# Attention, routed experts and a dense softplus layer on one core: a branch past the weight split of an expert block whose predecessor had the same expert

## The chip, the cores and the metric

One Trainium2 chip; the kernel runs on one core of it. The metric is the device time of one execution in microseconds (us), the median of repeated runs. The kernel before takes 573.91 us (three runs, 573.8 to 574.29).

## What is computed

Three stages follow each other; all inputs are float32.

```
a = attention(rotate(q), rotate(k), v)             # 2 batches, 8 heads, 576 tokens, 64 dims
x = a as [1152 tokens, 512]
e = argmax(norm(x) @ norm(expert_emb).T / tau)     # one of 8 experts per token
x[t] = gate[t] * (relu(x[t] @ w1[e]) @ w2[e])      # w1: 8 x 512 x 1024, w2: 8 x 1024 x 512
out = softplus(x @ w_in) @ w_out                   # 512 -> 2048 -> 512
```

For the inputs of the measurement the eight experts receive 109, 200, 97, 486, 143, 31, 85 and 1 tokens.

## The kernel before

TensorE multiplies fp32r numbers. To keep float32 accuracy every operand is split into a high part (its value rounded to fp32r, a copy on ScalarE) and a low part (the difference, on VectorE); each product is then three matmuls: high by high, high by low, low by high.

The expert stage (some 194 to 363 us of the span) sorts the tokens by expert into blocks of 128 rows. Every expert has at least one block and one more for each further 128 tokens; blocks of one expert are neighbours. With the counts above there are 13 blocks (`NU`, line 913), of experts 0, 1, 1, 2, 3, 3, 3, 3, 4, 4, 5, 6, 7. On the chip VectorE computes this sequence: `eid` is the expert of a block, and `chg` (line 299) is 1 where a block's expert differs from that of the block before it. So `chg` is 0 for blocks 2, 5, 6, 7 and 9.

Per block n the work is: gather the 128 rows, transpose and split them (`x_t`, `x_ev`), 24 matmuls of the first layer in four chunks of the contraction (`layer1`, line 1001), relu on ScalarE (line 1008), transpose and split the hidden rows (`h_t`, `h_ev`, line 985), 24 matmuls of the second layer in four chunks (`layer2`, line 1030), scale by the gate (`y_row`, line 1037) and scatter the rows to memory (`y_put`, line 1040).

Weights: the two layers have four raw chunks each of 128 x 1024 floats (`raws_w`, line 934), one buffer per layer and chunk. `fetch_w(n, l, c)` (line 943) issues on SyncE's queue the 512 KB transfer of chunk c of layer l for block n. It carries the condition `chg[n] > 0`, so for a block that repeats the expert no bytes move and the raw buffer keeps its data. `split_hi` (line 959) takes a buffer of the eight in pool `wp` and writes the high part on ScalarE (line 962); `split_lo` (line 964) writes the low part on VectorE (line 966) and then issues the fetch of the same chunk for block n + 1, which may overwrite the raw chunk as soon as both halves have read it. The splits are done for every block, whether its raw chunk is new or not.

All engines run in an order written out by hand. Blocks 0 to 3 are interleaved with the routing in straight code; from n = 4 the loop `run` (line 1066) holds a steady pattern. One turn n is, in the order of each engine's queue: split the hidden rows of block n - 1 (`h_ev`), `layer1(n)`, split the second layer's weights of block n - 1, `relu(n)`, the rows of block n + 1 (`x_t`, `x_ev`), `y_out(n - 2)`, split the first layer's weights of block n + 1, `layer2(n - 1)`, from n = 8 the transposes of one tile of finished rows for the next stage (`y_t`, line 903, whose load `y_load`, line 896, SyncE issues a turn earlier behind that turn's weight fetches), `h_t(n)`, and `between(n)`. For n = 4 to 7 `between` also decodes one chunk of the dense layer's weights on ScalarE and VectorE (`decode`, line 861), and fetches another. The lines of the loop that split weights:

```
                if n0 < n < n1:
                    for c in range(4):
                        split_w(n - 1, 1, c)
...
                    for c in range(4):
                        if (n + 1, 0, c) not in wts:
                            split_w(n + 1, 0, c)
```

After the loop a branch of all engines (lines 1292 and 1302) jumps past the code for a 14th to 16th block, which isn't needed here; then the dense stage runs.

Of the kernel before, what the change touches and what calls it, by code (L numbers as in the profile page):

```python
# [13 lines left out]
F32R = mybir.dt.float32r  # L14
# [11 lines left out]
P = 128  # L26
B, H, S, D = 2, 8, 576, 64
NT, DM = B * S, H * D
E, FF, DFF = 8, 1024, 2048
# [61 lines left out]
def f(ap):  # L91
    return ap.bitcast(F32)
# [3 lines left out]
def moe_kernel(ctx: ExitStack, tc: tile.TileContext, q, k, v, emb, tau, w1, w2, w_in, w_out, rope, tab, out):  # L96
    nc = tc.nc
# [51 lines left out]
    chg = rt.tile([P, NBLK], I32, name="chg")  # L149
# [699 lines left out]
    NB = NBLK  # L849
# [63 lines left out]
    NU = E + 5  # L913
# [5 lines left out]
    if True:  # L919
        wr = ectx.enter_context(tc.tile_pool(name="wr", bufs=1, reuse_waits="tile"))  # L920
        xg_ = ectx.enter_context(tc.tile_pool(name="xg", bufs=1, reuse_waits="tile"))
        wp = ectx.enter_context(tc.tile_pool(name="wp", bufs=8, reuse_waits="tile"))
# [5 lines left out]
        xgs = [xg_.tile([P, DM], F32R, name=f"xg{i}") for i in range(3)]  # L928
        for t in xgs:
            G.memset(f(t), 0.0)  # L930
        regs, wts, xts, hts, hs, yps = {}, {}, {}, {}, {}, {}

        wr.tile([P, 528], F32, name="below")
        raws_w = {(l, c): wr.tile([P, FF], F32, name=f"raw{l}{c}") for l in range(2) for c in range(4)}
# [8 lines left out]
        def fetch_w(n, l, c):  # L943

            if n >= NB:
                return
            if l == 0:
                src = w1.rearrange("e (k p) f -> e k p f", p=P)
            else:
                src = w2.rearrange("e (c p r) d -> e c p (r d)", p=P, r=2)  # L950
            if n == 0:
                SY.dma_start(raws_w[l, c], src[0, c])
                return
            if n not in regs:
                regs[n] = [SY.value_load(t[0:1, n:n + 1], min_val=0, max_val=m) for t, m in ((eid, E - 1), (chg, 1))]
            e, new = regs[n]
            SY.dma_start(raws_w[l, c], src[ds(e, 1), c].rearrange("e p f -> (e p) f"), cond=(new > 0) if (n, l) != (1, 0) else (e < 1))

        def split_hi(key):
            raw = raws_w[key[1:]]  # L960
            wt = wts[key] = wp.tile([P, 2, FF], F32R, tag="w", name="wt")
            A.copy(wt[:, 0], raw)  # L962

        def split_lo(key, eng=None, ahead=True):
            raw, wt = raws_w[key[1:]], wts[key]
            (eng or V).tensor_tensor(wt[:, 1], raw, f(wt[:, 0]), op=ALU.subtract)  # L966
            if ahead:
                fetch_w(key[0] + 1, *key[1:])

        def split_w(*key):  # L970
            split_hi(key)
            split_lo(key)

        def gather(n):
            G.indirect_dma_start(f(xgs[n % 3])[:, :], None, xs[:, :], bass.IndirectOffsetOnAxis(idx[:, n:n + 1], axis=0), bounds_check=NT - 1, oob_is_err=False)
# [11 lines left out]
        def x_t(n):  # L987
            return four(lambda k: xgs[n % 3][:, k * P:(k + 1) * P], F32R)

        def x_ev(n, pt, tag="xt"):  # L990
            xt = xts[n] = xe.tile([P, 2, 4, P], F32R, tag=tag, name="xt", bufs=1)
            hi_lo(xt, pt)

        def layer1(n):
            xt = xts.pop(n)
            ph = hs[n] = [ps_x.tile([P, 512], F32, tag="x", name="ph") if n == 1 else ps_h.tile([P, 512], F32, tag="h", name="ph") for _ in range(2)]
            for c in range(4):
                wt = wts.pop((n, 0, c)) if n else firsts.pop(c)
                for i in range(2):
                    for a, r in ((0, 0), (0, 1), (1, 0)):  # L1000
                        T.matmul(ph[i], lhsT=xt[:, a, c], rhs=wt[:, r, 512 * i:512 * i + 512] if n else wt[r][:, 512 * i:512 * i + 512], start=(c == 0 and a == 0 and r == 0), stop=(c == 3 and a == 1))  # L1001
                yield

        def relu(n):
            ph = hs.pop(n)
            h = hs[n] = xe.tile([P, FF], F32, tag="hr", name="hr", bufs=1)
            for i in range(2):
                A.activation(h[:, 512 * i:512 * i + 512].rearrange("p (k r q) -> p k r q", k=2, r=2), ph[i].rearrange("p (k q r) -> p k r q", k=2, r=2), AF.Relu)

        def h_t(n):  # L1010
            h = hs.pop(n)
            return [four(lambda k: h[:, 512 * i + P * k:512 * i + P * k + P]) for i in range(2)]

        def h_ev(n, pts, mid=lambda: None):
            ht = hts[n] = [xe.tile([P, 2, 4, P], F32R, tag=f"ht{i}", name="ht", bufs=1) for i in range(2)]
            for i in range(2):
                hi_lo(ht[i], pts[i])
                if i == 0:
                    mid()

        def layer2(n):
            ht = hts.pop(n)
            py = yps[n] = ps_y.tile([P, DM], F32, tag="y", name="py")
            for c in range(4):
                wt = wts.pop((n, 1, c))
                for r in range(2):
                    rhs = wt.rearrange("p a (r d) -> p a r d", r=2)[:, :, r]
                    k = 2 * (c % 2) + r
                    for a, s in ((0, 0), (0, 1), (1, 0)):
                        T.matmul(py, lhsT=ht[c // 2][:, a, k], rhs=rhs[:, s], start=(c == 0 and r == 0 and a == 0 and s == 0), stop=(c == 3 and r == 1 and a == 1))  # L1030
                yield
# [14 lines left out]
        def y_out(n):  # L1046
            y_row(n)
            y_put(n)
# [17 lines left out]
        def run(n0, n1, between=lambda n: None, early=lambda n: None, early_t=lambda n: lambda: None, pts=None):  # L1066

            for n in range(n0 if pts is None else n0 + 4, n1 + 1):
                if n + 2 < n1:
                    gather(n + 2)  # L1070
                if pts:
                    h_ev(n - 1, pts)
                    pts = None
                if n == n1:
                    split_w(n - 1, 1, 3)
                    if n0 + 2 <= n:
                        y_out(n - 2)
                    between(n)
                if n < n1:
                    for _ in layer1(n):  # L1080
                        pass
                if n0 < n < n1:
                    for c in range(4):
                        split_w(n - 1, 1, c)
                if n < n1:
                    relu(n)
                if n + 1 < n1:
                    px = x_t(n + 1)
                if n + 1 < n1:
                    x_ev(n + 1, px)  # L1090
                if n0 + 2 <= n < n1:
                    y_out(n - 2)
                if n + 1 < n1:
                    for c in range(4):
                        if (n + 1, 0, c) not in wts:
                            split_w(n + 1, 0, c)
                elif n < n1:
                    between(n)
                    split_w(n, 1, 0)
                l2 = layer2(n - 1) if n0 < n <= n1 else iter(())  # L1100
                if n + 1 == n1:
                    for _ in range(2):
                        next(l2, None)
                    h_ev(n, h_t(n), lambda: [split_w(n, 1, c) for c in (1, 2)])
                for _ in l2:
                    pass
                ev = early_t(n)
                if n + 1 < n1:
                    pts = h_t(n)
                ev()  # L1110
                if n == n1:
                    y_row(n - 1)
                if n < n1:
                    early(n)
                if n + 1 < n1:
                    between(n)

        def between(n):
            if n == 1:
                pgat = bank(2).rearrange("p a e -> p (a e)")  # L1120
                for b in range(B):
                    at_places(pgat, b, "row", "gm")
                V.tensor_copy(gates, pgat)
                xctx.close()
                ypool = ctx.enter_context(tc.tile_pool(name="ypool", bufs=1, side="right", reuse_waits="tile"))
                yr3.extend(ypool.tile([P, DM + 1], F32R, name=f"yr{i}") for i in range(4))
                ypools.append(ypool)
                for t in yr3:
                    G.memset(f(t), 0.0)
                yts[0] = ypool.tile([P, 2, 4, TOK_PASSES[0][1] * P], F32R, name="yt0")  # L1130
            if n in (2, 3):
                for i in range(2 * n - 4, 2 * n - 2):
                    fetch(*ORDER[i], raw_)
            if 4 <= n < 8:
                decode((*ORDER[n - 4], dec))
                fetch(*ORDER[n], raw_)
            if n == NU - 1:
                split(0, 0)
                tc.mark_branch_hint_location("extra", T.value_load(extra[0:1, 0:1], min_val=0, max_val=1), [mybir.EngineType.PE])
            if n == NU:  # L1140
                split(0, 1)
# [333 lines left out]
```

## Time and profile before

| | us |
|---|---|
| median of three runs | 573.91 |
| the profiled execution | 574.03 |
| its span | 572.3 |
| TensorE busy | 544.2 |
| VectorE busy | 448.8 |
| ScalarE busy | 440.1 |
| GpSimd busy | 202.6 |

The span runs from the first to the last instruction of the profiled execution; its own time is 1.73 us longer. Busy times are of the engines' own instructions and run beside each other; the share over the whole span hides that the stages have different limits, so the expert loop has to be read by itself.

### The profile page before, as it was taken

What the parts mean: (1) busy time and instruction counts of PE and PEld (TensorE: products, weight loads), DVE (VectorE), ACT (ScalarE), POOL (GpSimd) and SP (SyncE); (2) the same over time, 40 slices, a digit from 0 to 9 for tenths busy, and PEclk for the clock granted to TensorE, in tenths of its full rate; (3) what the DMA queues carried; (4) which work ended last, traced back from release to release, by engine and by line L of the source; (5) the groups of instructions that cost most, each with busy time, mean ns of one, the idle gap of its engine ahead of it and who ended that gap; (6) DMA issues with size and microseconds to landing.
All of it is one profiled execution on the core that took longest, in us unless ns stands there. A gap on an engine that the chain in (4) does not pass through costs nothing. (4 is left out here: it accounts for less than half of the span.)

```text
span 572.3 us, 10066 instructions
## 1 busy us (share of the span) xinstructions
PE 544.2 (95%) x3361; PEld 477.2 (83%) x3361; DVE 448.8 (78%) x747; ACT 440.1 (77%) x838; POOL 202.6 (35%) x314
## 2 busy tenths in 40 slices
PE   6799999999999999998999999899999999999995
PEld 6689899999988888887778888797889999888994
DVE  6788887878977779989999998687877766787243
ACT  4787878887775599799998988788877877676550
POOL 7999999849731420332222412300000000000033
PEclk9899999999999999999999999999999999999999
DMA  5405200061143655982539895453332222000012
GB/s 143 123 2 151 67 1 3 0 221 38 38 169 116 199 163 174 316 300 71 216 102 333 290 377 174 133 191 102 107 112 74 77 80 71 33 1 2 0 74 92
DMA packets 37431, 70.61 MB, mean 123 GB/s; under 512 B 8306, under 2 KB 24050, under 8 KB 37248
## 3 DMA queue, kind: packets, MB, share of 16 engines
q1 hardware_dynamic: 34400, 62.66, 33.1%
q0 software_dynamic: 2800, 7.09, 3.6%
q8 instruction: 28, 0.46, 0.3%
q10 hardware_dynamic: 176, 0.18, 0.2%
q14 instruction: 27, 0.22, 0.1%
HBM read 91.14 MB, written 8.13 MB: 173 GB/s over the span
## 5 line engine op out<-in xcount | busy, mean ns | idle before, releaser
L966 DVE TENSOR_TENSOR wt<-raw,wt 128x1024 fp32r<-128x1024 f32 x100 | 116.4, 1221 | 5.8 <-ACT wt L962 5.8
L1336 PE MATMUL ph<-yt,wt 128*128 128x320 f32 (+1 forms) x576 | 105.4, 336 | 2.5 <-ACT r__5876 L1348 1.4
L1383 PE MATMUL po<-wt,g 128*128 128x512 f32 x432 | 103.6, 391 | 0.0
L1336 PEld LDWEIGHTS ph<-yt,wt 128*128 128x128 f32 x576 | 93.5, 188 | 11.8 <-ACT r__5876 L1348 1.8
L962 ACT CAST wt<-raw 128x1024 fp32r<-128x1024 f32 x100 | 98.8, 1066 | 5.5 <-DMA raw<-in_moe_w_dram 5.5
L1383 PEld LDWEIGHTS po<-wt,g 128*128 128x128 f32 x432 | 80.4, 188 | 16.7 <-ACT g L1367 0.3
L1030 PE MATMUL py<-wt,ht 128*128 128x512 f32 x312 | 75.7, 395 | 3.8 <-DVE wt L966 3.8
L1400 POOL DMA_INDIRECT out_dram<-acc,otok x9 | 9.6, 1067 | 186.2 <-DVE acc L1397 185.6
L1030 PEld LDWEIGHTS py<-wt,ht 128*128 128x128 f32 x312 | 57.5, 188 | 16.6 <-DVE wt L966 5.1
L1001 PE MATMUL ph<-wt,xt 128*128 128x512 f32 x288 | 69.1, 394 | 0.0
L543 ACT ACTIVATE p<-sc,nm 128x576 f32<-128x576 f32 x72 | 54.0, 750 | 11.6 <-DVE nm L537 10.7
L1001 PEld LDWEIGHTS ph<-wt,xt 128*128 128x128 f32 x288 | 53.1, 188 | 10.6
L537 DVE TENSOR_REDUCE nm<-sc 128x1 f32<-128x576 f32 x72 | 54.1, 752 | 3.1 <-PE sc L533 1.9
L556 ACT CAST ph<-tp 128x512 fp32r<-128x512 f32 (+1 forms) x80 | 42.8, 547 | 13.5 <-PE tp L549 13.0
L533 PE MATMUL sc<-kt,qt 128*128 128x288 f32 x256 | 50.4, 319 | 0.8 <-ACT p L543 0.4
L567 DVE TENSOR_TENSOR pl<-tp,ph 128x512 fp32r<-128x512 f32 (+1 forms) x80 | 49.5, 628 | 0.1
L379 POOL TENSOR_TENSOR t<-qk,ropet 128x256 f32<-128x256 f32 x61 | 43.7, 744 | 10.6 <-DMA qk<-in_q_dram 10.2
L549 PE MATMUL tp<-idf,p 128*128 128x128 f32 x288 | 44.8, 278 | 1.8 <-DVE jz L233 0.6
L1367 ACT CAST g<-e 128x512 fp32r<-128x512 f32 (+2 forms) x33 | 21.6, 658 | 29.6 <-PE po L1383 20.2
L1368 DVE TENSOR_TENSOR g<-e,g 128x512 fp32r<-128x512 f32 (+2 forms) x33 | 24.3, 740 | 23.7 <-ACT g L1367 23.5
L594 PE MATMUL po<-ph,vs 128*128 128x288 f32 x128 | 36.4, 307 | 2.2 <-DVE p L435 1.3
L533 PEld LDWEIGHTS sc<-kt,qt 128*128 128x128 f32 x256 | 36.7, 192 | 1.8 <-ACT p L543 1.1
(246 smaller groups left out, 1001.7 us busy)
## 6 DMA issues: line engine op xcount, KB each, us to landing
raw<-in_moe_w_dram SPq DMA_DIRECT2D x116, 512.0 KB
raw<-in_moe_w_in_dram SPq DMA_DIRECT2D x16, 512.0 KB
raw<-in_moe_w_out_dram SPq DMA_DIRECT2D x16, 512.0 KB
yr<-ys SPq DMA_DIRECT2D x9, 256.5 KB
qk<-in_k_dram SPq DMA_DIRECT2D x8, 256.0 KB
qk<-in_q_dram SPq DMA_DIRECT2D x8, 256.0 KB
vv<-in_v_dram SPq DMA_DIRECT2D x8, 256.0 KB
xs<-xrow SPq DMA_DIRECT2D x1, 1024.0 KB
```

Of the source, the lines that this page charges most:

```text
L379: eng.tensor_tensor(t[:, i, g], x4[:, i, g], ropet[:, m, 0:4].unsqueeze(2).to_broadcast([P, 4, 2, 32]), op=ALU.mult)
L533: T.matmul(sc[:, n, 0:288], lhsT=w, rhs=r, start=(x == 0), stop=(x == len(mm) - 1))
L537: V.tensor_reduce(nm, tiles['sc', t][:, :, 0:288], axis=AX.XY, op=ALU.max, negate=True)
L543: A.activation(p.rearrange("p (n t) -> p n t", n=2), tiles.pop(('sc', t))[:, :, 0:288], AF.Exp, bias=tiles.pop(('nm', t)), accum_out=head( ...
L549: T.transpose(tp[:, x], p[:, x * P:x * P + P], idf)
L567: V.tensor_tensor(hd['pl'][:, :, sl], tp[:, :, x * w:x * w + w], f(hd['ph'][:, :, sl]), op=ALU.subtract)
L962: A.copy(wt[:, 0], raw)
L966: (eng or V).tensor_tensor(wt[:, 1], raw, f(wt[:, 0]), op=ALU.subtract)
L1001: T.matmul(ph[i], lhsT=xt[:, a, c], rhs=wt[:, r, 512 * i:512 * i + 512] if n else wt[r][:, 512 * i:512 * i + 512], start=(c == 0 and a == ...
L1030: T.matmul(py, lhsT=ht[c // 2][:, a, k], rhs=rhs[:, s], start=(c == 0 and r == 0 and a == 0 and s == 0), stop=(c == 3 and r == 1 and a == 1))
L1336: T.matmul(phs[i][:, 0:n1 - n0], lhsT=wt[:, a, k], rhs=yts[p][:, r, k, n0:n1], start=(k == 0 and a == 0 and r == 0), stop=(k == 3 and a == 1))
L1383: T.matmul(outs[i][c], lhsT=g[:, a, c * P:c * P + P], rhs=wt[:, r], start=(first and a == 0 and r == 0), stop=(last and a == 1))
```

## The change

A block with `chg` 0 uses the split weights of its predecessor. The eight split buffers get fixed places, one per layer and chunk (`held`), where before they rotated. In the loop the two calls go through `split_new`: it loads `chg[n]` into a register of VectorE and of ScalarE (once per block), and both engines branch on it past the four copies and the four subtractions of that layer. The four fetches for block n + 1 now stand behind the branch in program order instead of one behind each chunk. The branch stands for blocks 3 to 11 in the second layer and 5 to 12 in the first; the straight code ahead of the loop and the last block's second layer split as before.

```diff
@@ split_hi @@
         def split_hi(key):
             raw = raws_w[key[1:]]
-            wt = wts[key] = wp.tile([P, 2, FF], F32R, tag="w", name="wt")
+            home = (0 if key[0] in (NU - 1, NU, NB - 1) else key[1], key[2])
+            if home not in held:
+                held[home] = wp.tile([P, 2, FF], F32R, tag="w", name="wt")
+            wt = wts[key] = held[home]
             A.copy(wt[:, 0], raw)
@@ behind split_w @@
+        def split_new(n, l, cs):
+
+            if n >= NU or (n, l) in ((0, 1), (1, 0)):
+                for c in cs:
+                    split_w(n, l, c)
+                return
+            for c in cs:
+                wts[n, l, c] = held[l, c]
+            if n not in news:
+                news[n] = nc.values_load(chg[0:1, n:n + 1], engines=[mybir.EngineType.DVE, mybir.EngineType.Activation], min_val=0, max_val=1)
+            with tc.If(news[n] > 0, preferred_fallthrough_block=True):
+                for c in cs:
+                    split_hi((n, l, c))
+                    split_lo((n, l, c), ahead=False)
+            for c in cs:
+                fetch_w(n + 1, l, c)
@@ run @@
                 if n0 < n < n1:
-                    for c in range(4):
-                        split_w(n - 1, 1, c)
+                    split_new(n - 1, 1, range(4))
...
                 if n + 1 < n1:
-                    for c in range(4):
-                        if (n + 1, 0, c) not in wts:
-                            split_w(n + 1, 0, c)
+                    split_new(n + 1, 0, range(4))
```

## Rows read from the trace of the kernel before

**Rows 1.** The page: span, busy time of each engine, and one costly group of instructions.

```profile
span 572.3 us, 10066 instructions
...
PE 544.2 (95%) x3361; PEld 477.2 (83%) x3361; DVE 448.8 (78%) x747; ACT 440.1 (77%) x838; POOL 202.6 (35%) x314
...
L962 ACT CAST wt<-raw 128x1024 fp32r<-128x1024 f32 x100 | 98.8, 1066 | 5.5 <-DMA raw<-in_moe_w_dram 5.5
```

**Rows 2.** Block periods by window (loop n = 4 to 9): engines' busy time (x instructions), clock, DMA share, GB/s.

```profile
240.28:252.45 12.17, 12.17 (x64) 10.16 (x61) 10.11 (x12) 10.38 (x15) 5.05 (x6) 1.00 1.02 355
252.45:266.34 13.89, 12.46 (x64) 10.15 (x62) 13.68 (x16) 13.89 (x21) 4.20 (x5) 1.00 0.41 142
266.34:279.60 13.26, 12.44 (x63) 10.15 (x61) 13.05 (x17) 12.25 (x18) 3.62 (x4) 1.00 0.19 66
279.60:292.84 13.24, 12.46 (x64) 10.16 (x62) 13.04 (x17) 12.05 (x17) 3.35 (x4) 1.00 0.62 225
292.84:306.39 13.55, 12.76 (x67) 10.47 (x65) 13.35 (x17) 11.37 (x16) 3.48 (x4) 1.00 0.55 175
306.39:318.88 12.49, 12.49 (x67) 10.47 (x66) 12.49 (x14) 11.52 (x16) 2.78 (x3) 1.00 0.87 301
```

**Rows 3.** Waits of TensorE after 194 us: us in total, times, longest.

```profile
PE py L1030 <- DVE wt L966: 3.8, 4, 1.4
...
PE ph L1336 <- ACTq L1302: 1.1, 1, 1.1
```

**Rows 4.** Timeline of TensorE, second layer of block 4: start, us, engine, line.

```profile
258.29 0.47 PE L1030 MATMUL py<-wt,ht 128*128 128x512 f32 x1
260.19 5.51 PE L1030 MATMUL py<-wt,ht 128*128 128x512 f32 x23 [1.43 <-DVE wt L966]
```

**Rows 5.** Timeline of VectorE, loop n = 5 into n = 6.

```profile
258.93 4.66 DVE L966 TENSOR_TENSOR wt<-raw,wt 128x1024 fp32r<-128x1024 f32 x4
...
264.11 4.61 DVE L966 TENSOR_TENSOR wt<-raw,wt 128x1024 fp32r<-128x1024 f32 x4
...
270.99 0.68 DVE L985 TENSOR_TENSOR ht<-pt,ht 128x512 fp32r<-128x512 f32 x1
```

**Rows 6.** Source line 1302, the branch after the loop: ns min/median/max, first and last start.

```profile
L1302 SPq EVENT_SEMAPHORE  x9: 17/17/17, 361.0 to 361.6; - x9
...
L1302 DVEq COMPARE_BRANCH  x1: 72/72/72, 359.8 to 359.8; - x1
L1302 PEldq COMPARE_BRANCH  x1: 675/675/675, 360.2 to 360.2; - x1
...
L1302 SPq COMPARE_BRANCH  x1: 53/53/53, 360.5 to 360.5; - x1
...
L1302 ACTq COMPARE_BRANCH  x1: 45/45/45, 362.3 to 362.3; - x1
```

**Rows 7.** Source line 1292, the load of that branch's value into registers.

```profile
L1292 DVEq TENSOR_LOAD <-nblk x1: 542/542/542, 359.2 to 359.2; - x1
...
L1292 SPq FUSED_REGOPS  x1: 164/164/164, 360.2 to 360.2; - x1
...
L1292 ACTq TENSOR_LOAD <-nblk x1: 464/464/464, 361.8 to 361.8; - x1
```

**Rows 8.** Timeline of all engines, loop n = 9.

```profile
306.26 1.08 ACT L984 CAST ht<-pt 128x512 fp32r<-128x512 f32 x2
...
309.23 0.35 SPq L896 DMA_DIRECT2D yr<-ys  x1
310.12 4.63 DVE L966 TENSOR_TENSOR wt<-raw,wt 128x1024 fp32r<-128x1024 f32 x4
...
312.24 5.69 PE L1030 MATMUL py<-wt,ht 128*128 128x512 f32 x24
...
317.33 2.61 POOL L907 COPY otok<-yr 128x1 int32<-128x1 int32 x1 [1.68 <-DMA yr<-ys]
...
317.77 0.46 PE L903 MATMUL pt<-idr,yr 128*128 128x128 f32 x4
```

More of the change, by code (lines that the diff above doesn't have):

```diff
@@ L930, in moe_kernel @@
             G.memset(f(t), 0.0)
-        regs, wts, xts, hts, hs, yps = {}, {}, {}, {}, {}, {}
+        regs, wts, xts, hts, hs, yps, held, news = {}, {}, {}, {}, {}, {}, {}, {}
         wr.tile([P, 528], F32, name="below")
```

## The prediction

> **What bounds the kernel now.** I read the page first, then the expert loop turn by turn, then who kept TensorE waiting there. The page gives TensorE 95% of the span and VectorE 78% [rows 1]: over the whole kernel VectorE is no bound, and the shares alone would say that taking work from it is worth nothing. The turns say otherwise. A turn starts with the first matmul of `layer1(n)`. At n = 4 it lasts 12.17 us and TensorE is busy throughout; at n = 5, 6, 7 and 8 it lasts 13.89, 13.26, 13.24 and 13.55, though TensorE's busy time is the same 12.4 to 12.5 (at n = 8 some 0.3 more, the four transposes of a tile `yr`); at n = 9 it is 12.49 and full again [rows 2]. VectorE is busy 13.68 of 13.89 and 13.05 of 13.26 in the slow turns: there it sets the pace, because `decode` is added to the two weight splits. From n = 9 the decode is gone and TensorE is the bound. DMA has room in the slow turns (share 0.19 to 0.62) and little at n = 4 and 9 (1.02, 0.87).
>
> The list of waits names the place: `py` (second layer) waits four times for VectorE's `wt`, 3.8 us in all, beside 1.1 us for the branch at line 1302 behind the loop [rows 3]. The wait sits behind the first matmul of `layer2(n - 1)`: that one needs only the high part, the second needs the low part of chunk 0, which isn't there, so the next 23 start at 260.19 instead of some 0.24 after 258.29 [rows 4].
>
> **What is removed, and its worth.** `chg` is 0 for blocks 5, 6, 7 and 9, so eight of the loop's seventeen sets of four chunks go: first layer of 5, 6, 7, 9, second layer of the same. A set costs VectorE 4.61 to 4.66 us [rows 5], so about 8 x 4.63 = 37 us of it go, and on ScalarE at most 8 x 4 x 1.066 = 34 us [rows 1]. Nearly all of this is not on the path. What counts is which of the four waits it ends. In VectorE's queue the four are one chain: split of block n - 1, rows of n + 1, split of n + 1, decode, hidden rows of n, next split, with hardly a gap from 258.93 to 270.99 [rows 5].
> - Turn 5 waits for the split of block 4, second layer, which stays (4 is a new expert). But the set ahead of it in the queue, first layer of block 5 in turn 4, goes. The split then starts some 4.6 us sooner, or as soon as its hidden rows are ready; the wait to be covered is 1.7.
> - Turns 6, 7, 8 wait for blocks 5, 6, 7, whose sets go altogether, with one more set gone from the same chain each.
>
> So all four should end. Their worth by turns with the same TensorE work: 13.89 - 12.17 = 1.72, 13.26 - 12.17 = 1.09, 13.24 - 12.17 = 1.07 and, with the transposes in both, 13.55 - 12.49 = 1.06 [rows 2]; sum 4.94. The wait list has 3.8 [rows 3], because the lone matmul is drawn 0.47 long where its successor could start after 0.24 (4 x 0.24 = 1.0 more, in all 4.8). I take 4.94; 3.8 is the lower end. What is late next in those turns: nothing on VectorE or ScalarE, which keep about 13.05 - 9.3 = 3.8 us and 12.25 - 8.5 = 3.7 us of work in turn 6 [rows 1, 2, 5]. TensorE is late next, so the gain stops there, however much more is taken from the others.
>
> **What is added.** Ten register loads (blocks 3 to 12) and seventeen branches, each on two engines. No row shows a branch inside the loop; the nearest is the one behind it.
> - The test takes 0.045 us on ScalarE, 0.072 on VectorE, 0.675 on TensorE; on SyncE, which has no arithmetic to wait for, 0.45 us pass from the end of its test (360.5 + 0.05) to the first instruction at the target (361.0) [rows 6]. The load takes 0.54 us on VectorE and 0.46 on ScalarE, the register work behind it 0.16 [rows 7].
> - So a branch costs between nothing (done ahead while the engine works through what is queued) and 0.54 + 0.16 + 0.675 + 0.45 = 1.8 us. I take 0.7, nearest to the test of VectorE and the jump of SyncE with some of the load, and it is not on the path: for a skipped set it replaces 4.6 us.
> - For a set that is taken, the cover is the lead of the split. In turn 9 ScalarE has cast the hidden rows by 306.26 + 1.08 = 307.34; VectorE, once it has no backlog, follows with 0.68 and then the first chunk (4.63 / 4 = 1.16), done near 309.2; TensorE needs it at 312.24 + 0.24 = 312.5 [rows 5, 8]. Today VectorE starts that set only at 310.12. The lead is 3.3 us, more than 1.8. If the cover were gone, the price would be up to 1.8 for each of the nine taken sets.
>
> [...] The rows show a test of 0.045 to 0.675 us and 0.45 for a jump over a long body [rows 6]. [...]
>
> **What is moved.** The four fetches of a set stand behind the branch. On SyncE's queue their order is unchanged: nothing else stood between them. Each still waits for the reader of its raw chunk, so behind a taken set I cost the move at nothing, and if they waited for the whole set the first would leave up to 3 x 1.16 = 3.5 us later, before a use a whole turn off. Behind a skipped set they leave sooner, together. Queued behind them on SyncE is the load of the `yr` tile, for which TensorE's transposes wait: today it is issued at 309.23, lands at 317.33 and is used at 317.77, 0.44 us to spare [rows 8]. TensorE comes 4.94 sooner, to 312.83. If the load gains only what turns 5 to 7 give (3.88), it lands at 313.45 and costs 0.62; if the skipped set of turn 8 lets it go earlier still, nothing. I take nothing, because both sets of turn 8 go.
>
> Fixed buffers: from turn 4 on the rotation of eight gives each layer its own four anyway, so nothing.
>
> **Sum.** 574.03 - 4.94 = 569.09 for the profiled execution (span 567.4). It lies 0.12 above the median of the runs shown, so the median goes to 568.97; rounded, 569.0.
>
> **The rivals.**
> - *Part of the gain.* The wait of turn 5 stays (its own set isn't skipped; the chain may be held by something that the backlog hides, such as its raw chunks, since DMA is full through turn 4 [rows 2]), or a `yr` tile is late. 1.72 and 0.62 come back: 569.0 + 1.7 = 570.7, with both 571.3. Chance 0.10.
> - *No change.* Readers of a branched set wait for the whole of it, not for a chunk. Then the last chunk counts, 3 x 1.16 = 3.5 us after the first, against a lead of 3.3 in turn 9: 0.2 there, and in turns of less lead more. Nine sets are taken; at 0.55 each the 4.94 are gone: 573.9. For it: TensorE does wait for a branch at line 1302 [rows 3]. Against: that one is of all engines. A flag that never lets a set be skipped ends at the same time; against it, the fetches use this flag already, and turn 6 moves only 66 GB/s [rows 2]. Chance 0.07.
> - [...] Chance 0.06.
>
> **How the numbers follow.** The forecast has 0.77. A measurement of this kernel tells 0.2%, 1.15 us, from no change. The first two cases are faster: 0.77 + 0.10 = 0.87; same 0.07; slower 0.06. The range goes from 568.4 (the forecast less 0.6, half of the wait at line 1302 in case it shrinks too) to 571.5 (the part-gain rival with both its prices, and a little; the 3.8 of the wait list, 570.1, lies inside). It holds the forecast and the part-gain case, 0.87, less some 0.05 for what no row prices.
>
> **What would show it.** Right: the turns 5 to 8 last 12.2, 12.2, 12.2 and 12.5; `py` has no wait on `wt`; lines 962 and 966 have 68 instructions each instead of 100; VectorE idles in the gaps, some 37 us less busy. Wrong: waits of `ph` or `py` on `wt` in turns 9 to 12, with branch or load instructions of VectorE longer than 2 us ahead of them; or a wait of `pt` on the `yr` load; or 100 splits still there.

## The result and the profile after

The changed kernel takes 568.92 us (four runs, 568.4 to 569.29), the kernel before beside it 573.86. The ratio is 0.9912, interval 0.9895 to 0.9929: faster by 0.9%. The forecast was 569.0, the range 568.4 to 571.5. The profiled execution took 568.89, its span 567.1, 5.2 less than before.

From the page of the changed kernel: the span, the busy times and the groups of the two split instructions.

```profile
span 567.1 us, 10053 instructions
...
PE 543.4 (96%) x3361; PEld 477.7 (84%) x3361; DVE 414.4 (73%) x715; ACT 409.9 (72%) x806; POOL 199.3 (35%) x314
...
L969 DVE TENSOR_TENSOR wt<-raw,wt 128x1024 fp32r<-128x1024 f32 x68 | 79.6, 1222 | 5.6 <-ACT wt L965 5.1
...
L965 ACT CAST wt<-raw 128x1024 fp32r<-128x1024 f32 x68 | 67.5, 1064 | 5.6 <-DMA raw<-in_moe_w_dram 5.6
```

Both splits have 68 instructions, 32 fewer than the 100 of before (ScalarE's in [rows 1]): eight sets of four. VectorE is busy 34.4 us less and ScalarE 30.2 (the prediction had 37 and at most 34), TensorE the same. Some six sevenths of the work that was taken off VectorE bought nothing by itself. What it bought shows turn by turn, as in [rows 2]: the windows of turns 5 to 9, each from the first matmul of `layer1(n)`, with the same columns (TensorE, weight loads, VectorE, ScalarE, GpSimd, granted clock, DMA share, GB/s).

```profile
252.50:264.67 12.17, 12.17 (x64) 10.15 (x62) 9.08 (x12) 8.25 (x13) 3.99 (x5) 1.00 0.48 161
264.67:276.84 12.17, 12.17 (x63) 10.16 (x62) 4.23 (x7) 4.55 (x9) 2.31 (x2) 1.00 0.41 136
276.84:289.01 12.17, 12.17 (x64) 10.15 (x62) 5.76 (x7) 7.93 (x12) 2.24 (x3) 1.00 0.54 192
289.01:301.51 12.50, 12.50 (x68) 10.49 (x66) 4.92 (x9) 4.03 (x9) 3.17 (x4) 1.00 0.69 216
301.51:313.99 12.48, 12.48 (x67) 10.47 (x66) 11.31 (x12) 11.38 (x16) 4.41 (x4) 1.00 0.78 279
```

Turns 5 to 8 last 12.17, 12.17, 12.17 and 12.50, TensorE is busy throughout each, and turn 9 is as before. VectorE has work for 4.2 to 5.8 us in turns 6 to 8, where it had 13. From turn 4's start to the start of the last turn of the loop, n = 12, the kernel now takes 98.65 us (240.33 to 338.98), before 103.59 (240.28 to 343.87): 4.94 less. TensorE's waits after 194 us:

```profile
PE ph L1353 <- ACT r__5887 L1365: 1.1, 1, 1.1
PE ph L1353 <- ACTq L1319: 0.9, 1, 0.9
PE pt L903 <- DMA yr<-ys: 0.8, 3, 0.5
```

`py` no longer waits for `wt` [rows 3]; the branch behind the loop still costs 0.9, and the dense stage has its own waits. VectorE's timeline, turn 6, where [rows 5] had an unbroken chain:

```profile
265.13 1.29 DVE L1005 TENSOR_TENSOR ht<-pt,ht 128x512 fp32r<-128x512 f32 x2 [1.78 <-ACT ht L1004]
271.52 0.69 DVE L1005 TENSOR_TENSOR xt<-pt,xt 128x512 fp32r<-128x512 f32 x1 [5.10 <-ACT xt L1004]
272.94 0.43 DVE L875 TENSOR_SCALAR a<-a 128x512 f32<-128x512 f32 x1 [0.73 <-ACT a L870]
```

Its hidden rows and its block rows now wait for ScalarE, and ScalarE for TensorE (3.07 us ahead of the cast of `ht`, 4.20 ahead of the relu): VectorE has become a follower.

### The profile page after: what moved, and what is told of

Its sections match the earlier page's. It is cut to its first block, busy times and chain, and to the rows that moved or that the text cites. A ratio compares the mean times of both kernels' runs of the same rounds, so it can differ in the third digit from the quotient of the medians.

```text
span 567.1 us, 10053 instructions
## 1 busy us (share of the span) xinstructions
PE 543.4 (96%) x3361; PEld 477.7 (84%) x3361; DVE 414.4 (73%) x715; ACT 409.9 (72%) x806; POOL 199.3 (35%) x314
## 5 line engine op out<-in xcount | busy, mean ns | idle before, releaser
L969 DVE TENSOR_TENSOR wt<-raw,wt 128x1024 fp32r<-128x1024 f32 x68 | 79.6, 1222 | 5.6 <-ACT wt L965 5.1
L965 ACT CAST wt<-raw 128x1024 fp32r<-128x1024 f32 x68 | 67.5, 1064 | 5.6 <-DMA raw<-in_moe_w_dram 5.6
```

## The experiments

Intervals are of the ratio to the kernel before on the same chip. Differences of a few tenths between variants are read from turns, not from medians.

**The same skips without branches** (`e1_static`).

```diff
-            if n not in news:
-                news[n] = nc.values_load(chg[0:1, n:n + 1], ...)
-            with tc.If(news[n] > 0, preferred_fallthrough_block=True):
+            if n not in (5, 6, 7, 9):
                 for c in cs:
```

> The change without its branches: no flag is loaded, no engine branches, and the program itself leaves out the splits of blocks 5, 6, 7 and 9, which are the skipped ones for these inputs. Theory (the branches lie beside other work, the gain is the end of four waits of TensorE): the same time as the changed kernel, 568.9 +- 0.4, turns 5 to 8 of 12.17, 12.17, 12.17, 12.49. Rival (the branches cost something on the path, and the waits were worth more than 4.94): faster than the changed kernel by 0.7 us or more, 568.2 or less.

Ratio 0.9923 (0.9904 to 0.9942), median 569.15; turns 5 to 8 as in the changed kernel (12.17, 12.17, 12.16, 12.50). Leaving the branches out gains nothing (569.15 against 568.92), so they lie beside other work. This program was even a little slower in its profiled execution, 570.32, by something else: the branch of all engines behind the loop, for which TensorE waits 2.0 us instead of 0.9. First that wait, then TensorE's test there, in the static program:

```profile
PE ph L1351 <- PEq L1317: 2.0, 1, 2.0
```

```profile
L1317 PEldq COMPARE_BRANCH  x1: 3655/3655/3655, 355.0 to 355.0; - x1
```

The test takes 3.66 us where it took 0.68 in [rows 6] and 0.94 in the changed kernel. It belongs to neither theory and comes back below.

**First layer only, second layer only** (`e3_first_only`, `e4_second_only`).

```diff
-            if n >= NU or (n, l) in ((0, 1), (1, 0)):
+            if n >= NU or l == 1 or (n, l) in ((0, 1), (1, 0)):      # e3: second layer always split
+            if n >= NU or l == 0 or (n, l) in ((0, 1), (1, 0)):      # e4: first layer always split
```

> Only the first layer's splits are branched past (blocks 5, 6, 7, 9); the second layer's are made for every block. Theory (a turn with four splits fewer leaves VectorE below TensorE's pace, and turn 5 needs block 5's first layer gone): no wait of py on wt in turns 5 to 8, 568.9 to 569.3, with half the splits skipped. Rival (each skipped set carries its share of the gain, 4.94 / 8 = 0.62): 571.4.

> Only the second layer's splits are branched past (blocks 5, 6, 7, 9). Theory: turn 5 keeps its wait, since nothing ahead of block 4's second-layer split is gone, 1.7 us; turns 6 to 8 lose theirs: 570.6. Rival (each set its share): 571.4; one wait list tells them apart: theory one wait of py on wt, rival several shorter ones.

With the first layer alone: 0.9907 (0.9889 to 0.9924), median 568.52, no wait of `py`, turns 5 to 8 of 12.17, 12.17, 12.17 and 12.50. Half the skips give the whole gain. With the second layer alone: 0.993 (0.9913 to 0.9948), median 569.53, and one wait:

```profile
PE py L1050 <- DVE wt L969: 1.0, 1, 1.0
```

It is in turn 5, which lasts 13.49; turns 6 to 8 are at TensorE's pace. The rival of equal shares is out on both counts. Turn 5's wait was smaller than expected, 1.32 over a clean turn instead of 1.72; more on that below.

**One set of the eight** (`e0_one_set`).

```diff
-            with tc.If(news[n] > 0, preferred_fallthrough_block=True):
+            if (n, l) != (5, 0):
```

> One set of the eight is skipped, the first layer of block 5, by the program itself, without branches; all others are split. Theory (what counts is how far VectorE is ahead of TensorE, and one set gone puts it some 4.6 us ahead, which later turns use up at 13.26 - 12.17 = 1.09 each): no wait of py on wt in turns 5 and 6, about none in 7, one of some 1.3 in turn 8, so most of the gain from one set: 570.3. Rival (a set is worth its share, 0.62, or turn 5's wait alone, 1.7): 573.3 or 572.2.

Turns 5 to 8 (same columns):

```profile
252.72:264.89 12.17, 12.17 (x64) 10.15 (x62) 10.29 (x11) 11.41 (x16) 3.37 (x5) 1.00 0.45 156
264.89:277.06 12.17, 12.17 (x63) 10.16 (x62) 11.97 (x15) 12.14 (x17) 3.33 (x2) 1.00 0.24 76
277.06:290.09 13.03, 12.47 (x64) 10.15 (x62) 12.83 (x16) 12.27 (x18) 3.88 (x4) 1.00 0.63 231
290.09:303.64 13.55, 12.77 (x67) 10.48 (x66) 13.35 (x17) 11.37 (x16) 3.46 (x4) 1.00 0.50 156
```

Turns 5 and 6 are clean, turn 7 is 0.86 longer than a clean turn and turn 8 is 1.05 longer. VectorE, put ahead once, loses its lead turn by turn and is the pace again two turns later, as the theory has it, though the wait comes back one turn earlier than forecast. From turn 4's start to the start of turn 9 this kernel takes 63.09 us (240.55 to 303.64), the kernel before 66.11 [rows 2]: one set in eight gave 3.0 of 4.94. Turn 9 then lasts 12.81 (303.64 to 316.45) instead of 12.49, because its `yr` tile lands late (at 315.20), so at the start of turn 12 2.7 are left. The median doesn't settle it: 572.18, ratio 0.9985 (0.9966 to 1.0003), its executions spread from 570.2 to 575.5, and in the profiled one TensorE's test behind the loop took 3.44 us again.

**Branches that are never followed past the splits.** The first try (`e2_all_taken`) changed the test to one that is always true:

```diff
-            with tc.If(news[n] > 0, preferred_fallthrough_block=True):
+            with tc.If(news[n] > -1, preferred_fallthrough_block=True):
```

> The branches stay and are never followed past the splits: the test is made true for either value of the flag, so all seventeen sets are split. Theory (a taken branch lies beside the work of its engine, a few tenths at most): turns 5 to 8, where VectorE sets the pace and nothing hides its losses, are as before the change plus 0.0 to 0.2 per branch, eight branches: 573.9 to 575.5. Rival (0.7 us for each branch that is taken, as the prediction priced it): 573.9 + 8 x 0.7 = 579.5.

A miss as a test of branches: the loaded value is declared to be 0 or 1, so that test is always true, and the trace has no branch in the loop (nothing on line 987, where the changed kernel has 26 branch instructions on each of the two engines). It has VectorE's ten loads (0.30 to 0.55 us each), the fetches behind the whole set and the fixed buffers; ScalarE's loads are gone as well. Ratio 0.999 (0.998 to 1.0001), turns 5 to 7:

```profile
252.22:265.39 13.17, 12.47 (x63) 10.15 (x62) 12.95 (x15) 13.17 (x20) 3.15 (x4) 1.00 0.43 149
265.39:278.63 13.24, 12.45 (x64) 10.16 (x62) 13.04 (x17) 12.21 (x18) 3.80 (x4) 1.00 0.19 66
278.63:291.84 13.21, 12.44 (x63) 10.15 (x62) 13.01 (x16) 12.04 (x17) 3.73 (x4) 1.00 0.59 225
```

So VectorE's loads, the fetch order and the buffers cost nothing, even where VectorE sets the pace: turns 6 and 7 last 13.24 and 13.21, against 13.26 and 13.24 in [rows 2]. The second try (`e8_branch_taken`) loads a value that VectorE writes as 1 for every block:

```diff
+        V.tensor_scalar(one, ef, 0.0, None, op0=ALU.is_ge)
...
-                news[n] = nc.values_load(chg[0:1, n:n + 1], ...)
+                news[n] = nc.values_load(one[0:1, n:n + 1], ...)
```

> All seventeen branches stay in the program and none is followed past the splits: the register gets a value that VectorE writes as 1 for every block, by one small instruction more in the routing. Theory (a branch lies beside its engine's queued work even where VectorE sets TensorE's pace): turns 6 and 7 of 13.2 to 13.6 against 13.26 and 13.24 before the change, and 572.8 to 574.5. Rival (0.7 us a branch, the prediction's price): two branches a turn in four turns, 8 x 0.7 = 5.6 more, turns of 14.6, 579.

Ratio 1.0002 (0.9991 to 1.0013). The windows of turns 5 to 8, then VectorE's branch instructions of that line (ns, shortest, median, longest):

```profile
252.40:265.44 13.04, 12.53 (x64) 10.15 (x61) 12.82 (x16) 12.48 (x18) 3.04 (x3) 1.00 0.39 140
265.44:278.62 13.18, 12.48 (x63) 10.15 (x62) 12.98 (x16) 12.69 (x19) 4.31 (x4) 1.00 0.26 83
278.62:291.88 13.26, 12.51 (x64) 10.16 (x62) 13.06 (x17) 12.04 (x17) 3.91 (x4) 1.00 0.64 224
291.88:305.38 13.50, 12.78 (x67) 10.48 (x66) 13.29 (x17) 11.37 (x16) 3.40 (x4) 1.00 0.54 159
```

```profile
L989 DVEq COMPARE_BRANCH  x34: 43/47/55, 242.9 to 348.3; - x34
```

There are two for each of the seventeen sets, the test and a jump at the end of the body. Turns 6 and 7 last 13.18 and 13.26, against 13.26 and 13.24 before [rows 2]: with four branch instructions a turn on the engine that sets the pace, nothing is lost. VectorE's instructions also start within 0.02 us of those of `e2_all_taken`, which has no branches, from 257.97 to 314.29. The price of 0.7 is out; on the path it is 0.0 within 0.08 a turn. One turn of this run is longer than before, turn 9 with 13.13 (305.38 to 318.51) against 12.49: its `yr` load left 0.4 us later than in `e2_all_taken` (308.79 against 308.38), behind a row scatter that was issued at the same time in both (by 302.05) and landed later, and TensorE was ready before the tile. So that loss sits at a transfer and not at VectorE; why the scatter took longer was not tested.

**A delay in every taken set** (`e5_late1`, `e6_late3`): chunk 0's low part is computed two or four times, which makes VectorE late by 1.16 or 3.5 us in each of the nine taken sets.

```diff
                 for c in cs:
                     split_hi((n, l, c))
-                    split_lo((n, l, c), ahead=False)
+                    for _ in range(2 if c == 0 else 1):      # e6: 4
+                        split_lo((n, l, c), ahead=False)
```

> The changed kernel with the low part of chunk 0 computed twice in every set that is taken: each such set ends its first chunk 1.16 us later on VectorE, as a branch that costs 1.16 would make it. Theory (lead of 1.75 us at block 3, some 3 us elsewhere, less the first set's delay for the second set of a turn): no wait but about 0.4 us in turn 12, 568.9 to 569.6. Rival (no cover): nine sets x 1.16 = 10.4 more, 579.3.

> [...] Theory with the leads of the changed kernel's trace (block 3 1.7, block 4 0.5, block 8 0.6 and 0.5, block 10 2.1 and 0.8, block 11 0.4 and 2, block 12 2): 579.5. Rival (no cover): nine sets x 3.5 = 31 more, 600.

With 1.16: ratio 0.9974 (0.9962 to 0.9986), median 571.93, some 3 us worse than the changed kernel, where the theory had 0.4. Up to turn 11 nothing is lost: turn 4's start to turn 12's start is 98.73 us, the changed kernel's 98.65, so eight of the nine sets have their delay covered. What is lost is lost in turn 12, which holds the ninth, that of block 11's second layer: from its start to the dense stage's first matmul it is 22.1 us (338.88 to 360.97) instead of 18.8 (338.98 to 357.76). Its timeline with the delay, then in the changed kernel:

```profile
343.82 5.88 DVE L969 TENSOR_TENSOR wt<-raw,wt 128x1024 fp32r<-128x1024 f32 x5
...
346.35 2.80 PE L1051 MATMUL py<-wt,ht 128*128 128x512 f32 x11 [1.53 <-DVE wt L969]
346.42 11.90 SPq L957 DMA_DIRECT2D raw<-in_moe_w_dram  x8
...
350.05 1.05 ACT L965 CAST wt<-raw 128x1024 fp32r<-128x1024 f32 x1 [3.75 <-DMA raw<-in_moe_w_dram]
```

```profile
341.22 4.63 DVE L969 TENSOR_TENSOR wt<-raw,wt 128x1024 fp32r<-128x1024 f32 x4
342.57 9.43 SPq L957 DMA_DIRECT2D raw<-in_moe_w_dram  x7
...
346.30 1.06 ACT L965 CAST wt<-raw 128x1024 fp32r<-128x1024 f32 x1
```

VectorE begins that set 2.7 us later in relation to its turn (343.82 against 341.22, with turns that start at 338.88 and 338.98), mostly, it seems, because the delay of turn 11's two sets (2 x 1.16) is still with it; TensorE waits 1.53. The fetch of block 12's second layer leaves behind that set (346.42 against 342.57), ScalarE gets the raw chunk only at 350.05 (346.30), and TensorE loses 1.1 us more behind it. In all other turns a fetch has a turn to land; this one is used in the turn in which it is issued.

With 3.5: ratio 1.0329 (1.0301 to 1.0357), median 592.89, 24 us worse than the changed kernel. The 579.5 was far too low. TensorE's waits for VectorE:

```profile
PE py L1051 <- DVE wt L969: 10.9, 5, 4.0
PE ph L1022 <- DVE wt L969: 3.2, 3, 2.0
PE py L1051 <- DVEq L987: 0.9, 1, 0.9
```

Together they are 10.9 us in five waits and 3.2 in three, in turns 4, 5 and 8 to 12, the longest 4.02 in turn 11 and 3.71 in turn 12. The last line is a set that is skipped, in turn 8: TensorE waits there until VectorE's queue, late by the set ahead of it, has come to the branch. So turns other than 9 and 11, the two with two taken sets each, lose time as well. But 15.0 us are not yet 24. Much of the rest is another thing: after the longest waits, 1.91 to 4.02 us, TensorE's clock is lower for a while. The windows of turn 4 of this kernel (the granted clock is the number ahead of the DMA share):

```profile
240.44:248.65 8.21, 6.30 (x32) 4.99 (x31) 8.11 (x10) 7.47 (x12) 3.77 (x4) 1.00 0.98 334
248.65:250.50 1.85, 1.85 (x7) 1.47 (x8) 1.85 (x2) 1.40 (x3) 0.92 (x1) 0.83 0.49 113
250.50:252.50 2.00, 2.00 (x6) 1.55 (x5) 2.00 (x3) 0.00 (x0) 1.70 (x2) 0.50 0.96 324
252.50:256.42 3.92, 3.92 (x22) 3.28 (x20) 2.34 (x5) 0.16 (x1) 0.60 (x2) 0.90 0.99 391
```

TensorE is idle for 1.91 us at the end of the first. The clock then falls within the second window (0.83 is a mean), is 0.50 of full speed in the third and rises again within the fourth (a mean of 0.90); in turn 5, from 256.42 on, it is 1.00. The 23 matmuls behind that wait take 7.14 us instead of 5.51, those behind the waits of 1.96 and 4.02 take 7.12 and 8.42, and the 11 behind the wait of 3.71 take 4.38 instead of the 2.80 of `e5_late1`: 7.7 us more in all. With the waits that is 22.7, and with some 0.24 in front of each of the nine waits, which the wait list leaves out as the prediction says, nearly all of the 25.5 us between the two profiled executions (594.37 and 568.89). Over turns 5 to 8 of the kernel before, with waits of at most 1.4 us [rows 3], the clock stayed at 1.00 [rows 2]. The length of the wait alone seems not to decide it: the 48 matmuls behind the branch that follows the loop took 7.27 us after a wait of 1.73 in `e0_one_set`, against 7.31 after 0.88 in the changed kernel, and the wait of 2.0 us there in `e1_static` cost no more than itself: the span is 1.1 longer than the changed kernel's (568.2 against 567.1), as the wait is (2.0 against 0.9). What makes the difference was not tested.

**Spending the freed time** (`e7_decode_early`, beside `c0_change`, the changed kernel itself): a fifth `decode` and the first split of the dense layer go into turn 8, and the dense stage begins with one decode instead of two.

```diff
-NPRE = 4
+NPRE = 5
...
-            if 4 <= n < 8:
+            if n == 8:
+                split(0, 0)
+            if 4 <= n < 9:
                 decode((*ORDER[n - 4], dec))
+            if 4 <= n < 8:
                 fetch(*ORDER[n], raw_)
             if n == NU - 1:
-                split(0, 0)
...
-                new = [(*x, gp) for x in ORDER[done_:done_ + (2 if u == 0 else 1)]]
+                new = [(*x, gp) for x in ORDER[done_:done_ + 1]]
```

> The changed kernel itself, for a comparison on one chip with the next: 0.9912 of the kernel before, turns 5 to 8 of 12.17, 12.17, 12.17 and 12.50 us.

> The changed kernel with one chunk of the dense layer's weights decoded a turn earlier: a fifth decode in turn 8, where VectorE and ScalarE now idle some 7 us, and one instead of two in the first step of the dense stage; the first split of the dense stage moves to turn 8 too. Theory (the freed time can be spent: ScalarE sets the pace from the end of the loop to the wait of the matmuls of the fourth hidden chunk, 1.1 us in the changed kernel's trace, and a decode is 1.3 us of it): that wait shrinks to under 0.4 and the time by 0.7 to 1.1 against the changed kernel beside it. Rival (the second pass's rows, which land from memory just then, set that stretch): no change, within 0.3.

The changed kernel: 0.9915 (0.99 to 0.993), median 568.67, turns 5 to 8 again 12.17, 12.17, 12.17 and 12.50. With the early decode: 0.9895 (0.9878 to 0.9912), median 567.64, all five runs below all six of the other, so this version is faster than both kernels. TensorE's waits behind the loop, in the changed kernel, then with the early decode:

```profile
PE ph L1353 <- ACT r__5887 L1365: 1.3, 1, 1.3
PE ph L1353 <- ACTq L1319: 0.9, 1, 0.9
```

```profile
PE ph L1355 <- ACTq L1321: 1.2, 1, 1.2
PE ph L1355 <- ACT r__5887 L1367: 0.9, 1, 0.9
```

The wait for ScalarE's `r` falls by 0.4 only, less than forecast. From the start of turn 12 to the matmuls behind it the two profiled executions take 43.97 us (339.08 to 383.05) and 43.51 (338.47 to 381.98). So about half of the 1.0 us is shown where it was looked for. The other 0.6 lies ahead of turn 4 in these two executions (240.43 against 239.80; from turn 4 to turn 12 they take 98.65 and 98.67), where the edit moves no work, and that it is an effect of the edit is not shown.

## Why the prediction was right

**The bound and where it sits.** Right. The page's shares said that VectorE was no bound; four turns said that it was. `e8_branch_taken`, with all the work of before, shows the four waits again (2.7 us in all, the longest 0.7), and the changed kernel none.

**4.94 us.** Right in the sum: the loop got shorter by 4.94 and the median by 4.94. That both agree to the hundredth is luck: the interval allows 4.1 to 6.0 us, and `c0_change`, the same kernel on another chip, gained 4.60. One term is not as fixed as it was put. Turn 5 with its wait lasted 13.89 before, 13.49 with the second layer alone, 13.17 and 13.04 with all sets split: 0.9 to 1.7 over a clean turn. In these executions ScalarE's `yo` of turn 4, which waits for the scatter of the row block before it and stands ahead of block 5's split, began 8.84, 8.43, 8.12 and 7.98 us into the turn (before, `e4_second_only`, `e2_all_taken`, `e8_branch_taken`); turn 5 was longer than a clean one by 1.72, 1.32, 1.00 and 0.87, in each case 7.1 less than that start. So the size of this wait goes with the landing of that scatter, which the prediction didn't have; no run varied it alone.

**Which sets count.** The prediction said that turn 5 owes its end to the set ahead in the queue, block 5's first layer, and turns 6 to 8 to two gone sets each. The first half is shown by `e4_second_only` (that set present, the wait stays) and by `e0_one_set` (that set alone gone, the wait goes). The second half asked for too much, and in turn 8 the set just ahead of block 7's second layer is block 8's first, which stays. In `e3_first_only` one set is gone in turns 5, 6 and 8, and none in turn 7, and no wait is left: VectorE is busy 8.98 and 8.90 us of 12.17 in turns 5 and 6, and 10.39 in turn 7, which the lead from the turns ahead covers.

**The branches.** Bounded at 0 to 1.8, taken as 0.7, off the path. In the changed kernel (columns as in [rows 6]):

```profile
L987 ACTq COMPARE_BRANCH  x26: 34/39/55, 241.2 to 339.8; - x26
L987 DVEq COMPARE_BRANCH  x26: 43/50/69, 243.0 to 343.8; - x26
L987 DVEq EVENT_SEMAPHORE  x8: 21/21/21, 248.8 to 316.4; - x8
```

Seventeen tests and nine further branches, one for each taken set, all of 34 to 69 ns on ScalarE and VectorE, and eight semaphore instructions of 21 ns on VectorE, one for each skipped set. `e1_static` (569.15 without branches, 568.92 with them) and `e8_branch_taken` (turns 6 and 7 of 13.18 and 13.26, against 13.26 and 13.24 in [rows 2]) show the price on the path: none.

**The cover.** The lead of the taken sets was put at 3.3 us in turn 9. Its timeline now:

```profile
303.43 4.64 DVE L969 TENSOR_TENSOR wt<-raw,wt 128x1024 fp32r<-128x1024 f32 x4
...
304.88 0.33 SPq L896 DMA_DIRECT2D yr<-ys  x1
...
307.35 5.69 PE L1050 MATMUL py<-wt,ht 128*128 128x512 f32 x24
...
311.44 0.86 POOL L907 COPY otok<-yr 128x1 int32<-128x1 int32 x1 [0.71 <-DMA yr<-ys]
...
312.88 0.46 PE L903 MATMUL pt<-idr,yr 128*128 128x128 f32 x4
```

The first chunk is done at 303.43 + 4.64 / 4 = 304.6, and TensorE needs it at 307.35 + 0.24 = 307.6: 3.0. The set ends at 308.07, after TensorE has begun to use it, and TensorE didn't wait: readers behind the branch wait chunk by chunk, so the rival of waits for a whole set is out. `e5_late1` shows that 1.16 us a set is covered in every turn but the last.

**The `yr` load.** I took nothing between 0 and 0.62, because the skipped sets of turn 8 would let the fetches ahead of the load go. The load now leaves at 304.88, lands at 311.44 and is used at 312.88: 1.4 us to spare instead of 0.44. The result is right and the reason is not. The fetches did leave sooner, the last of them by 293.63 + 7.14 = 300.8 instead of 308.9, but the load then stood for something else, the scatter of block 6's rows to the memory that it reads:

```profile
293.63 7.14 SPq L957 DMA_DIRECT2D raw<-in_moe_w_dram  x8
```

```profile
SPq L896 <- DMA ys<-yo,dest: 3.8, 1, 3.8
```

It left 4.35 us sooner, while its turn began 4.88 sooner (301.51 against 306.39 [rows 2]). What saved it is that it landed 6.56 us after it left, not 8.10 [rows 8]; why is not shown, so the zero was in part luck. In `e0_one_set` and `e8_branch_taken`, where it took 8.1 and 8.5, turn 9 was 0.3 and 0.6 longer: the rival's late tile is real, at up to the size that the prediction gave it.

**The part-gain rival** named raw chunks behind a full DMA. They were late: ScalarE's last copy of block 4's second layer waits 0.68 us for its chunk (changed kernel).

```profile
256.94 1.06 ACT L965 CAST wt<-raw 128x1024 fp32r<-128x1024 f32 x1 [0.68 <-DMA raw<-in_moe_w_dram]
```

TensorE uses that chunk last and didn't notice.

**Slower.** The prediction has a chance of 0.06 for a slower kernel. No run shows what would make it so: the loop's branches took 34 to 69 ns each, and the load of the flag at most 0.55 us. What a price of some us would do is shown by the delays: with 3.5 us in each taken set the kernel is 3.3% slower than before, and with 1.16 it has lost 3 us and is still 0.3% below it, so the delay that brings it back to the time of before lies between 1.2 and 3.5 us a set. Three things add to the loss at 3.5: turns 4, 5, 8 and 10 waited too, not only those with two taken sets, the last turn's fetch has no turn to land, and the longest waits cost again in clock (0.50 behind 1.91 us).

## What to carry to other kernels

Read the bound turn by turn: an engine with a 78% share can set the pace in four turns of thirteen, and then it is the lead of one engine over the next that is bought, not busy time; one set placed ahead of the slow stretch gave 3.0 of 4.94 us in that stretch, half of the sets all of it. A short branch around work of one engine was free here (34 to 69 ns, and turns of 13.18 and 13.26 against 13.26 and 13.24), even in the turns where that engine set the pace; look at the last turn of a loop by itself, where a load may be used in the turn that issues it. Work taken off an engine beyond what ended the waits was worth something here only once other work was put in its place, and of the 1.0 us that this gave, half could be placed.

## What was not expected

- After the four longest waits of `e6_late3`, 1.91, 1.96, 4.02 and 3.71 us, TensorE's granted clock was 0.50, 0.57, 0.50 and 0.62 over windows of 2.0 to 3.6 us; the first cost another 1.63 (7.14 us for matmuls that take 5.51). After the waits of at most 1.4 in the kernel before it stayed at 1.00, and the wait of 2.0 in `e1_static` cost no more than itself.
- TensorE's test in the branch of all engines behind the loop took 0.50 to 1.06 us in eight traces, and 3.44 and 3.66 in two, `e0_one_set` and `e1_static`, where TensorE then waited 1.7 and 2.0 us for it instead of 0.9 to 1.3. Neither has a branch inside the loop, but the kernel before and `e2_all_taken` have none either, and took 0.68 and 0.58. Why these two programs have the longer test was not shown.
- The test `news[n] > -1`, of a value declared to be 0 or 1, left no branch in the loop of `e2_all_taken`: nothing on line 987, where the changed kernel has 52 branch instructions.
